# Set-up of a convolution and mixer kernel: the weight on 32 partitions, and iotas between the first two loads of x

## The chip, the cores and the metric

One core of a Trainium2 chip runs the kernel. The metric is the device time of one execution in microseconds, the median of several executions; lower is better.

## The reference

The reference is a light-weight convolution followed by a low-rank token mixer and a two-layer channel mixer. It is cut here to what is computed.

```python
# x: (8, 4224, 192) f32, weight: (8 heads, 7 taps) f32
w = exp(weight - weight.max(-1, keepdims=True))
w = w / (w.sum(-1, keepdims=True) + 1e-9)             # softmax over the 7 taps
out[b, s, h, g] = sum_k w[h, k] * x_pad[b, s + k, h, g]    # causal, 6 zeros in front, 24 channels a head
x = out                                                # (8, 4224, 192)
h = x.transpose(0, 2, 1) @ U @ V                       # U: (4224, 32), V: (32, 4224)
u = x + h.transpose(0, 2, 1)
ch = maximum(u @ w_ch1, 0.0) @ w_ch2                   # 192 -> 768 -> 192
return u + ch
```

## The kernel before, in words

**The steady part.** x is loaded batch by batch and cast to bf16 on the way. TensorE convolves it: for each head it multiplies by a banded 64 or 32 column matrix that holds the softmax of the taps (`conv`, `conv32`). It then sums with U (`tt_mm`), adds the product with V, and runs the two layers of the channel mixer on groups of eight tiles of 128 tokens (`w1`, line 587, and `w2`, line 614). ScalarE and VectorE take the results out of PSUM. The order of the whole program is written out by hand (`SLOTS`, `LOADS`); each engine runs its instructions in program order.

**The set-up.** The change is in the set-up alone, which covers about the first 10 us. It has three strands that meet in the first convolution.

- *Loads.* SyncE issues the load of `weight` into `w_sb` (line 61), the same 56 numbers on every partition. GpSimd issues the first pieces of x for batch 0: `x_piece(0)` makes two transfers, part r = 0 for partitions 0 to 63 (480 KB as bf16) and part r = 1 for partitions 64 to 127 (504 KB), both at line 79. U, the other pieces of x, V and the mixer's weights are issued behind them on GpSimd's queue.
- *The bands.* GpSimd makes four index patterns with `iota` (lines 104 and 114): `dif`, `tap`, `fp` and `efp`. VectorE adds the quarter's offset `rq` to `dif` (line 180), takes the maximum of `w_sb` over the taps (`mx_sb`, 184) and the difference (`d_sb`, 186). ScalarE makes the exponential (193). VectorE compares `dif` with `tap` (`hot`, 195), makes the identity from `fp` (`ident`, 202), finishes the softmax (206 to 212) and multiplies it into the pattern (`pr`, 222, two halves of four heads). TensorE sums each half over the taps with the identity (`band_half`, line 246), and ScalarE (first half) and VectorE (second half) copy the sums into the two `bands`.
- *TensorE's filler.* `idle(4)`, four float32 matmuls of zeros (line 163), runs ahead of the first `band_half`, and `idle(1, 2)` between the two halves.

The first convolution follows at line 379. Its matmuls go r = 0, r = 0, r = 1, r = 1, and so on for each head, so the third of them needs the second transfer of x and the lower half of the first band. `x_zero(0, ...)` clears 64 partitions of row 0 of the tile of x; the convolution reads them as the zeros in front of the sequence.

VectorE also makes `Eq` (line 231) from `efp` and a second column of `rq`, which holds -4 times the first, and `R4` from `fp`; they serve the layout of U (line 274) and later sums.

Of the kernel before, what the change touches and what calls it, by code (L numbers as in the profile page):

```python
# [7 lines left out]
ALU = mybir.AluOpType  # L8
ACT = mybir.ActivationFunctionType
BF16 = mybir.dt.bfloat16  # L10
F32 = mybir.dt.float32
# [3 lines left out]
def kernel(  # L15
# [10 lines left out]
    nc = tc.nc  # L26
    P = nc.NUM_PARTITIONS
    B, S, D = x.shape
    H, KC = weight.shape
# [11 lines left out]
    QB = 32  # L41
# [3 lines left out]
    cst = ctx.enter_context(tc.tile_pool(name="cst", bufs=1))  # L45
# [10 lines left out]
    def bank():  # L56
        return psp.tile([P, 512], F32, name="ps", tag="ps")


    w_sb = cst.tile([P, H, KC], F32, name="w_sb")  # L60
    nc.sync.dma_start(out=w_sb[:], in_=weight[:].partition_broadcast(P))
    xt = [None] * B
    yt = [None] * B

# [5 lines left out]
    def x_tile(b):  # L70
        xt[b] = xs.tile([P, NB1 + 1, D], BF16, name="x_sb")

    def x_zero(b, eng):
        eng.memzero(xt[b][0:HB, 0, :])

    def x_part(b, r, s0, s1):

        blk = NB0 * r + s0 - 1
        return nc.gpsimd.dma_start(  # L79
            out=xt[b][HB * r : HB * r + HB, s0:s1, :],  # L80
            in_=x[b, blk * HB : (blk + s1 - s0) * HB, :].rearrange("(j p) d -> p j d", p=HB),
        )
# [2 lines left out]

    KP = [{0: (0, 10), 1: (0, 10)}, {1: (10, NB1 // 2)}, {0: (10, NB0 // 2)}]

    def x_piece(k):
        for r, (k0, k1) in KP[k].items():
            x_part(0, r, (1 - r if k0 == 0 else 2 * k0 + 1), 2 * k1 + 1)  # L90

    def piece_tiles(k):
        return [NB0 // 2 * r + j for r, ks in KP[k].items() for j in range(*ks)]

    x_tile(0)
    x_piece(0)


    I32 = mybir.dt.int32
# [3 lines left out]
    def iota(t, pattern, base, mul):  # L103
        nc.gpsimd.iota(
            t, pattern=pattern, base=base, channel_multiplier=mul,
            allow_small_or_imprecise_dtypes=True,
        )

    dif = cst.tile([P, BW], F32, name="dif")
    iota(dif[:], [[1, BW]], 0, -1)  # L110
    tap = cst.tile([P, KC], F32, name="tap")
    iota(tap[:], [[-1, KC]], HW, 0)
    fp = cst.tile([P, P], I32, name="fp")
    nc.gpsimd.iota(fp[:], pattern=[[1, P]], base=P, channel_multiplier=-1)
    efp = cst.tile([P, 4, P], F32, name="efp")
    iota(efp[:], [[-1, 4], [1, P]], 0, -4)

# [6 lines left out]
        out=Ur[:, 0:nfull, :], in_=U4[0 : nfull * P, :].rearrange("(k p) c -> p k c", p=P)  # L124
# [3 lines left out]
    for k in range(1, len(KP)):  # L128
        x_piece(k)
# [5 lines left out]
    for q in range(4):  # L135
        src = moe_V[:, 0 : full * 8 * P].rearrange("r (k q t) -> r k q t", q=4, t=2 * P)
        nc.gpsimd.dma_start(
            out=V_sb[32 * q : 32 * q + 32, 0 : 2 * full, :].rearrange(
                "r (k a) t -> r k (a t)", a=2
            ),  # L140
            in_=src[:, :, q, :],
        )
    W1_sb = cst.tile([P, 3, M4], BF16, name="W1_sb")
    for hf in range(2):
        nc.gpsimd.dma_start(
            out=W1_sb[HB * hf : HB * hf + HB, :, :],
            in_=moe_w_ch1[:, :].rearrange("(c k) m -> k c m", k=HB),
# [2 lines left out]
    zz = cst.tile([P, P], F32, name="zz")  # L150
    nc.vector.memzero(zz[:])  # L151

    rq = cst.tile([P, 2], F32, name="rq")
    for r in range(4):
        nc.vector.memset(rq[QB * r : QB * r + QB, 0:1], float(QB * r))
    nc.vector.tensor_scalar(
        out=rq[:, 1:2], in0=rq[:, 0:1], scalar1=-4.0, scalar2=None, op0=ALU.mult
    )
    wps = bank()

    def idle(n, w=4):
# [14 lines left out]
    bands = [cst.tile([P, HQ, P], BF16, name=f"band{hh}") for hh in range(2)]  # L176
    for hh in range(2):
        nc.vector.memzero(bands[hh][:])
    x_zero(0, nc.vector)
    nc.vector.tensor_scalar(  # L180
        out=dif[:], in0=dif[:], scalar1=rq[:, 0:1], scalar2=None, op0=ALU.add
    )
    mx_sb = cst.tile([P, H], F32, name="mx_sb")
    nc.vector.tensor_reduce(out=mx_sb[:], in_=w_sb[:], axis=mybir.AxisListType.X, op=ALU.max)
    d_sb = cst.tile([P, H, KC], F32, name="d_sb")
    nc.vector.tensor_tensor(
        out=d_sb[:],
        in0=w_sb[:],
        in1=mx_sb[:].unsqueeze(2).to_broadcast([P, H, KC]),
        op=ALU.subtract,  # L190
    )
    e_sb = cst.tile([P, H, KC], F32, name="e_sb")
    nc.scalar.activation(e_sb[:], d_sb[:], ACT.Exp)
    hot = cst.tile([P, KC, BW], BF16, name="hot")
    nc.vector.tensor_tensor(
        out=hot[:],
        in0=dif[:].unsqueeze(1).to_broadcast([P, KC, BW]),
        in1=tap[:].unsqueeze(2).to_broadcast([P, KC, BW]),
        op=ALU.is_equal,
    )  # L200
    ident = cst.tile([P, P], BF16, name="ident")
    nc.vector.tensor_scalar(
        out=ident[:], in0=fp[:], scalar1=float(P), scalar2=None, op0=ALU.is_equal
    )
    s_sb = cst.tile([P, H], F32, name="s_sb")
    nc.vector.tensor_reduce(out=s_sb[:], in_=e_sb[:], axis=mybir.AxisListType.X, op=ALU.add)
# [6 lines left out]
        out=c_sb[:].rearrange("p k h -> p h k"),  # L213
        in0=e_sb[:],
        in1=rs_sb[:].unsqueeze(2).to_broadcast([P, H, KC]),
        op=ALU.mult,
    )
    prs = []
    for hh in range(2):
# [3 lines left out]
            out=pr[:],  # L223
            in0=hot[:].unsqueeze(2).to_broadcast([P, KC, HQ, BW]),
            in1=c_sb[:, :, HQ * hh : HQ * hh + HQ].unsqueeze(3).to_broadcast([P, KC, HQ, BW]),
            op=ALU.mult,
# [2 lines left out]

    Eq = cst.tile([P, 4, P], BF16, name="Eq")  # L230
    nc.vector.tensor_scalar(
        out=Eq[:], in0=efp[:], scalar1=rq[:, 1:2], scalar2=None, op0=ALU.is_equal
    )

    nc.vector.tensor_scalar(
        out=fp[:], in0=fp[:], scalar1=R - 1, scalar2=None, op0=ALU.bitwise_and
# [3 lines left out]
        out=R4[:], in0=fp[:], scalar1=0.0, scalar2=None, op0=ALU.is_equal  # L240
# [493 lines left out]
    for r, (k0, k1) in KP[2].items():  # L734
        j = NB0 // 2 * r + k0
        nc.gpsimd.tensor_copy(
            out=U4_sb[:, o : o + k1 - k0, :, :],
            in_=U_sb[:]
# [8 lines left out]
        out=V_sb[0:32, 2 * (NT // 8), :], in_=moe_V[:, (NT - 1) * P : NT * P]  # L747
# [35 lines left out]
    for r in range(4):  # L783
        q = slice(QB * r, QB * r + QB)
        for hh in range(2):
            nc.gpsimd.tensor_copy(
                out=band2[q, HQ * hh : HQ * hh + HQ, :],
                in_=bands[hh][q, :, HB * (r % 2) : HB * (r % 2) + QB],
# [34 lines left out]
    for gs1, gs2, at in SLOTS:  # L823
# [13 lines left out]
        for p in range(npc + 1):  # L837
            for what in at.get(p, []):
                do(what)
            if p < npc:  # L840
                g, k = gs2[p // 4], p % 4
# [35 lines left out]
```

## Time and profile before

| | us |
|---|---|
| median of 3 executions | 324.3 (324.24 to 325.69) |
| the profiled execution | 324.34 |
| its span in the profile | 322.4 |
| TensorE busy | 316.4 (98% of the span) |
| VectorE busy | 268.9 (83%) |
| ScalarE busy | 169.6 (53%) |
| GpSimd busy | 141.8 (44%) |
| mean rate of the transfers | 166 GB/s |

Times in the profile are microseconds from the start of the span unless marked ns. PE is TensorE's matmul, PEld its weight load, DVE VectorE, ACT ScalarE, POOL GpSimd and SP SyncE; POOLq and SPq are the queues that issue transfers. A group in the timeline gives its start, its busy time, the engine, the line, the operation, what it writes and reads, the count, and in brackets the idle time ahead of it with what ended it. The profiled execution takes 1.94 us more than its span.

### The profile page before, as it was taken

The page shows a single profiled execution, that of the slowest core. Times are in us where ns is not written, and L with a number is a line of the kernel's source. Part 1 is how long each engine was busy: PE and PEld are TensorE (multiplying, and loading weights), DVE is VectorE, ACT ScalarE, POOL GpSimd, SP SyncE. Part 2 cuts the span into 40 slices and gives each one's busy share as a digit, 9 for nine tenths or more (in the row PEclk, how much of TensorE's full clock was granted, in tenths as well). Part 3 has the DMA queues.
Part 4 walks back from the last instruction along what each step waited for, and adds up shares of the span by engine and source line. Part 5 has one row for each costly group of instructions (what it writes and reads, how often), then busy time and mean ns, then how long its engine had stood idle before and what let it go on. Part 6 is the DMA issues. An engine that isn't in the chain of part 4 may idle for free.

```text
span 322.4 us, 9590 instructions
## 1 busy us (share of the span) xinstructions
PE 316.4 (98%) x4004; PEld 223.3 (69%) x4004; DVE 268.9 (83%) x550; ACT 169.6 (53%) x344; POOL 141.8 (44%) x108
## 2 busy tenths in 40 slices
PE   8999999999999999999999999999999999999996
PEld 3757576478678647867864884687797497487495
DVE  6769989987977986997898699789888897896864
ACT  1766723960874397088249609824903902912910
POOL 8763299429937983992897497000000000000000
PEclk9999999999999999999999999999999999999999
DMA  8999994999997999799689966138269059039035
GB/s 103 191 195 169 200 226 104 213 179 243 190 188 142 266 151 191 151 185 190 170 230 187 188 171 173 51 107 232 59 177 264 3 148 292 5 97 291 7 121 174
DMA packets 122442, 53.38 MB, mean 166 GB/s; under 512 B 87712, under 2 KB 122400, under 8 KB 122400
## 3 DMA queue, kind: packets, MB, share of 16 engines
q1 hardware_dynamic: 84528, 38.08, 47.4%
q0 software_dynamic: 37728, 14.60, 39.3%
q8 instruction: 31, 0.51, 0.7%
q10 hardware_dynamic: 144, 0.10, 0.1%
q14 instruction: 11, 0.09, 0.1%
HBM read 29.22 MB, written 25.95 MB: 171 GB/s over the span
## 4 chain that ended last, share of the span: by engine, by line
PE 91%; ACT 4%; DMA 2%; DVE 2%; issue 1%; POOL 0%; POOLq 0%
PE ps L614 42%; PE ps L587 39%; PE ps L349 3%; PE ps L469 3%; DMA x_sb<-in_x_dram 2%; PE ps L412 2%; ACT rl_sb L601 2%; ACT y_sb L266 2%; PE ps L379 1%; DVE u_sb L492 1%; DVE rl_sb L603 1%; PE ps L438 0%; PE ps L534 0%; POOL x_sb L79 0%; DVE out_sb L623 0%
## 5 line engine op out<-in xcount | busy, mean ns | idle before, releaser
L601 ACT ACTIVATE rl_sb<-ps 128x512 bf16<-128x512 f32 x233 | 124.3, 604 | 107.7 <-PE ps L587 95.7
L614 PE MATMUL ps<-W_sb,rl_sb 128*128 128x192 bf16 x1584 | 141.2, 246 | 0.2
L614 PEld LDWEIGHTS <-rl_sb 128*128 128x128 bf16 x1584 | 128.3, 98 | 11.8 <-issue 11.4
L587 PE MATMUL ps<-uT,W_sb 64*128 64x512 bf16 x1188 | 131.7, 376 | 0.3 <-DVE uT L268 0.2
L603 DVE TENSOR_SCALAR rl_sb<-ps 128x512 bf16<-128x512 f32 x163 | 105.3, 687 | 14.9 <-PE ps L587 14.7
L587 PEld LDWEIGHTS <-W_sb 64*128 64x128 bf16 x1188 | 66.8, 94 | 60.7 <-issue 4.0
L623 DVE TENSOR_TENSOR out_sb<-ps,u_sb 128x384 f32<-128x384 f32 (+1 forms) x133 | 70.3, 549 | 25.5 <-PE ps L614 25.0
L315 POOL COPY xb_sb<-x_sb 32x3072 bf16<-32x3072 bf16 (+1 forms) x24 | 67.7, 2822 | 1.1
L492 DVE TENSOR_TENSOR u_sb<-y_sb,ps 128x192 bf16<-128x192 bf16 (+1 forms) x168 | 66.2, 460 | 0.0
L303 POOL COPY xb_sb<-x_sb 128x3072 bf16<-128x3072 bf16 x12 | 32.9, 2744 | 39.5 <-PE ps L349 32.4
L266 ACT ACTIVATE y_sb<-ps 128x384 bf16<-128x384 f32 (+4 forms) x90 | 38.3, 519 | 9.8 <-PE ps L349 7.4
L79 POOL DMA_DIRECT2D x_sb<-in_x_dram x32 | 27.1, 853 | 13.9 <-PE ps L469 7.7
L268 DVE CAST y_sb<-ps 128x408 bf16<-128x408 f32 (+4 forms) x36 | 19.1, 577 | 1.4 <-PE ps L379 1.3
L469 PE MATMUL ps<-tt_sb,V_sb 32*128 32x192 bf16 x264 | 12.4, 246 | 0.1
L349 PE MATMUL ps<-x_sb,band 64*32 64x384 bf16 x192 | 12.1, 333 | 0.0
L349 PE MATMUL ps<-xb_sb,band 64*32 64x384 bf16 x192 | 12.1, 332 | 0.0
L469 PEld LDWEIGHTS <-V_sb 32*128 32x128 bf16 x264 | 4.7, 92 | 7.3 <-issue 7.3
L426 ACT ACTIVATE tt_hi<-ps 128x192 bf16<-128x192 f32 x8 | 2.6, 331 | 11.9 <-PE ps L412 11.9
L379 PE MATMUL ps<-x_sb,band 64*64 64x240 bf16 (+3 forms) x192 | 7.9, 275 | 0.5 <-DMA x_sb<-in_x_dram 0.4
L349 PEld LDWEIGHTS <-band 64*32 64x32 bf16 x384 | 4.5, 89 | 5.2 <-issue 2.4
L163 PE MATMUL ps<-zz 128*128 128x512 f32 (+1 forms) x10 | 6.5, 804 | 1.1 <-DVE zz L151 1.1
L379 PEld LDWEIGHTS <-band 64*64 64x64 bf16 x192 | 6.0, 106 | 2.2 <-issue 1.6
(65 smaller groups left out, 67.9 us busy)
## 6 DMA issues: line engine op xcount, KB each, us to landing
out_dram<-out_sb SPq DMA_DIRECT2D x131, 192.0 KB, 2.7
x_sb<-in_x_dram POOLq DMA_DIRECT2D x14, 384.0 KB, 7.6
x_sb<-in_x_dram POOLq DMA_DIRECT2D x7, 432.0 KB, 8.3
x_sb<-in_x_dram POOLq DMA_DIRECT2D x7, 408.0 KB, 7.8
W_sb<-in_moe_w_ch_dram POOLq DMA_DIRECT2D x3, 288.0 KB, 7.5
x_sb<-in_x_dram POOLq DMA_DIRECT2D x1, 504.0 KB, 7.5
uT<-u_sb SPq DMA_TRANSPOSE x31, 4.2
x_sb<-in_x_dram POOLq DMA_DIRECT2D x1, 480.0 KB, 5.7
```

Of the source, the lines that this page charges most:

```text
L79: return nc.gpsimd.dma_start(out=xt[b][HB * r : HB * r + HB, s0:s1, :], in_=x[b, blk * HB : (blk + s1 - s0) * HB, :].rearrange("(j p) d -> ...
L266: nc.scalar.activation(out=out, in_=in_, func=ACT.Copy)
L303: nc.gpsimd.tensor_copy(out=xbt[b][:, s0:s1, :], in_=xt[b][:, s0 + 1 : s1 + 1, :])
L315: nc.gpsimd.tensor_copy(out=xbt[b][q, s0:s1, :], in_=xt[b][q, s0:s1, :])
L349: nc.tensor.matmul(out=pp[r][QB * cg : QB * cg + QB, 0 : nk[r] * GS], lhsT=w[hr], rhs=t[hr, st : st + 2 * nk[r] - 1 : 2, hs], start=True, ...
L469: last = nc.tensor.matmul(out=banks[pr][:, a * D : (a + 1) * D], lhsT=V_sb[32 * q : 32 * q + 32, (j // 8) * 2 + j % 2, :], rhs=ttb[b][32 * ...
L492: nc.vector.tensor_tensor(out=u_group(g)[:, i : i + n, :, hf, :], in0=yt[b][:, run[0] : run[0] + n, :].rearrange("p n (c k) -> p n c k", c=3),
L587: last = nc.tensor.matmul(out=pps[m][hf][:], lhsT=W1_sb[HB * hf : HB * hf + HB, c, m * P : (m + 1) * P], rhs=uTt[g][HB * hf : HB * hf + HB ...
L601: nc.scalar.activation(out=rl[:, m, hf, :], in_=pp[hf][:], func=ACT.Relu)
L603: nc.vector.tensor_scalar_max(out=rl[:, m, hf, :], in0=pp[hf][:], scalar1=0.0)
L614: last = nc.tensor.matmul(out=cps[:, a * D : (a + 1) * D], lhsT=rlt[g][:, m, hf, (i + a) * P : (i + a + 1) * P], rhs=W2_sb[:, m, :], start ...
L623: nc.vector.tensor_tensor(out=o[:, 0:n, :].rearrange("p n (c k) -> p n c k", c=3), in0=cps[:, 0 : n * D].rearrange("p (n c k) -> p n c k", ...
```

## The change

The load of `weight` goes to 32 partitions instead of 128. The maximum runs on 32 partitions. The subtraction is written four times, each time from the same 32 partitions into one quarter of `d_sb`. The two first transfers of x are no longer issued back to back: between them GpSimd makes `fp`, `dif` and `tap` (now in this order) and clears the row of zeros, which VectorE did before; `efp` stays behind both. On VectorE the identity moves ahead of the maximum, and the addition to `dif` moves behind the subtractions. The second column of `rq` goes, with the instruction that made it; `Eq` multiplies by -0.25 in its own instruction and compares with the first column.

```diff
-    w_sb = cst.tile([P, H, KC], F32, name="w_sb")
-    nc.sync.dma_start(out=w_sb[:], in_=weight[:].partition_broadcast(P))
+    w_sb = cst.tile([QB, H, KC], F32, name="w_sb")
+    nc.sync.dma_start(out=w_sb[:], in_=weight[:].partition_broadcast(QB))
...
-    def x_piece(k):
+    def x_piece(k, rs=(0, 1)):
         for r, (k0, k1) in KP[k].items():
+            if r not in rs:
+                continue
             x_part(0, r, (1 - r if k0 == 0 else 2 * k0 + 1), 2 * k1 + 1)
...
     x_tile(0)
-    x_piece(0)
+    x_piece(0, (0,))
...
+    fp = cst.tile([P, P], I32, name="fp")
+    nc.gpsimd.iota(fp[:], pattern=[[1, P]], base=P, channel_multiplier=-1)
     dif = cst.tile([P, BW], F32, name="dif")
     iota(dif[:], [[1, BW]], 0, -1)
     tap = cst.tile([P, KC], F32, name="tap")
     iota(tap[:], [[-1, KC]], HW, 0)
-    fp = cst.tile([P, P], I32, name="fp")
-    nc.gpsimd.iota(fp[:], pattern=[[1, P]], base=P, channel_multiplier=-1)
+    x_zero(0, nc.gpsimd)
+    x_piece(0, (1,))
     efp = cst.tile([P, 4, P], F32, name="efp")
     iota(efp[:], [[-1, 4], [1, P]], 0, -4)
...
-    rq = cst.tile([P, 2], F32, name="rq")
+    rq = cst.tile([P, 1], F32, name="rq")
     for r in range(4):
         nc.vector.memset(rq[QB * r : QB * r + QB, 0:1], float(QB * r))
-    nc.vector.tensor_scalar(
-        out=rq[:, 1:2], in0=rq[:, 0:1], scalar1=-4.0, scalar2=None, op0=ALU.mult
-    )
...
-    x_zero(0, nc.vector)
+    ident = cst.tile([P, P], BF16, name="ident")
+    nc.vector.tensor_scalar(
+        out=ident[:], in0=fp[:], scalar1=float(P), scalar2=None, op0=ALU.is_equal
+    )
+    mx_sb = cst.tile([QB, H], F32, name="mx_sb")
+    nc.vector.tensor_reduce(out=mx_sb[:], in_=w_sb[:], axis=mybir.AxisListType.X, op=ALU.max)
+    d_sb = cst.tile([P, H, KC], F32, name="d_sb")
+    for r in range(4):
+        nc.vector.tensor_tensor(
+            out=d_sb[QB * r : QB * r + QB, :, :],
+            in0=w_sb[:],
+            in1=mx_sb[:].unsqueeze(2).to_broadcast([QB, H, KC]),
+            op=ALU.subtract,
+        )
+    e_sb = cst.tile([P, H, KC], F32, name="e_sb")
+    nc.scalar.activation(e_sb[:], d_sb[:], ACT.Exp)
     nc.vector.tensor_scalar(
         out=dif[:], in0=dif[:], scalar1=rq[:, 0:1], scalar2=None, op0=ALU.add
     )
-    mx_sb = cst.tile([P, H], F32, name="mx_sb")
...
-    d_sb = cst.tile([P, H, KC], F32, name="d_sb")
-    nc.vector.tensor_tensor(
-        out=d_sb[:],
-        in0=w_sb[:],
-        in1=mx_sb[:].unsqueeze(2).to_broadcast([P, H, KC]),
-        op=ALU.subtract,
-    )
...
     hot = cst.tile([P, KC, BW], BF16, name="hot")
...
-    ident = cst.tile([P, P], BF16, name="ident")
...
     Eq = cst.tile([P, 4, P], BF16, name="Eq")
     nc.vector.tensor_scalar(
-        out=Eq[:], in0=efp[:], scalar1=rq[:, 1:2], scalar2=None, op0=ALU.is_equal
+        out=Eq[:],
+        in0=efp[:],
+        scalar1=-0.25,
+        scalar2=rq[:, 0:1],
+        op0=ALU.mult,
+        op1=ALU.is_equal,
     )
```

More of the change, by code (lines that the diff above doesn't have):

```diff
@@ L182 @@
     )
-    mx_sb = cst.tile([P, H], F32, name="mx_sb")
-    nc.vector.tensor_reduce(out=mx_sb[:], in_=w_sb[:], axis=mybir.AxisListType.X, op=ALU.max)
-    d_sb = cst.tile([P, H, KC], F32, name="d_sb")
-    nc.vector.tensor_tensor(
-        out=d_sb[:],
-        in0=w_sb[:],
-        in1=mx_sb[:].unsqueeze(2).to_broadcast([P, H, KC]),
-        op=ALU.subtract,
-    )
-    e_sb = cst.tile([P, H, KC], F32, name="e_sb")
-    nc.scalar.activation(e_sb[:], d_sb[:], ACT.Exp)
     hot = cst.tile([P, KC, BW], BF16, name="hot")
@@ L199 @@
         op=ALU.is_equal,
-    )
-    ident = cst.tile([P, P], BF16, name="ident")
-    nc.vector.tensor_scalar(
-        out=ident[:], in0=fp[:], scalar1=float(P), scalar2=None, op0=ALU.is_equal
     )
```

## The prediction

> **What bounds the kernel now.** I read the head of the page first, for the whole; then the chain of waits over the first 40 us, because the change touches only the set-up; then the timeline of the first 14 us, to see what stands beside that chain; last the transfers in the first 10 us.
>
> ```profile
> span 322.4 us, 9590 instructions
> PE 316.4 (98%) x4004; PEld 223.3 (69%) x4004; DVE 268.9 (83%) x550; ACT 169.6 (53%) x344; POOL 141.8 (44%) x108
> ```
>
> TensorE is busy for 98% of the span. Nothing behind the set-up changes, so whatever the set-up gains or loses shifts the end by that much, and by no more. The chain in order of time (start, length, what) says what the set-up waits for:
>
> ```profile
> 1.26 1.02 POOL x_sb L79
> 2.29 7.50 DMA x_sb<-in_x_dram
> 9.79 0.04 issue
> 9.83 0.53 PE ps L379 x12
> ```
>
> The second transfer of x (r = 1) is issued at 2.29 and lands at 9.79; the convolution goes on at 9.83. The bands, on which most of the edits bear, are not on the chain. The timeline shows by how little:
>
> ```profile
> 0.75 0.40 SPq L61 DMA_DIRECT2D w_sb<-in_weight_dram  x1
> 1.07 5.90 PE L163 MATMUL ps<-zz 128*128 128x512 f32 x8 [1.07 <-DVE zz L151]
> 3.55 0.85 DVE L180 TENSOR_SCALAR dif<-dif,rq 128x38 f32<-128x38 f32 x1 [1.39 <-POOL dif L104]
> 3.74 0.62 POOL L104 IOTA efp<- 128x512 f32 x1
> 4.03 0.37 DVE L184 TENSOR_REDUCE mx_sb<-w_sb 128x8 f32<-128x56 f32 x1
> 6.05 2.44 DVE L222 TENSOR_TENSOR pr<-hot,c_sb 128x1064 bf16<-128x1064 bf16 x2
> 7.37 0.62 PE L246 MATMUL ps<-pr,ident 128*128 128x152 bf16 x7 [0.39 <-DVE pr L222]
> 9.10 0.29 PE L379 MATMUL ps<-x_sb,band 64*64 64x240 bf16 x2
> 9.83 1.83 PE L379 MATMUL ps<-x_sb,band 64*64 64x240 bf16 x62 [0.44 <-DMA x_sb<-in_x_dram]
> ```
>
> The first two matmuls of the convolution run at 9.10, as soon as the upper half of the first band is there; the other 62 stand until 9.79. The bands are ready about 0.6 us before the data.
>
> The transfers from 0 to 10 us, in 40 slices of 0.25 us:
>
> ```profile
> DMA  0000000000004899999999999999999999999999
> GB/s 0 0 0 0 0 0 0 18 20 19 16 4 53 68 99 104 106 158 195 190 190 187 195 183 178 177 184 175 184 197 195 192 192 195 190 188 175 182 183 183
> q1 hardware_dynamic: 144, 0.03, 1.2%
> ```
>
> The slices from 1.75 to about 3 us hold only the weight: the same view cut at 3.0 us has 94 of its 144 packets, cut at 3.7 us it has all. x begins at about 3.0 and needs until 4.5 to come to some 187 GB/s; from there the engines are full. The two transfers of x go one behind the other: part r = 0 lands at 6.96 (5.7 us after its issue, by the page), part r = 1 2.83 us later, and its 504 KB (516 thousand bytes) over 2.83 us are 182 GB/s, the full rate.
>
> **The two transfers of x with the iotas between them.** Part r = 0 is issued at 1.26 as before. Between them come three iotas and the clearing. The starts of `dif`, `tap`, `fp` and `efp` in the trace (3.31, 3.45, 3.55, 3.74) give 0.14 + 0.10 + 0.19 = 0.43 us; GpSimd's own clearing of that shape takes 0.20 at 12.74, and some 0.09 lies ahead of the first iota. The second issue moves from 2.29 to about 3.0. That costs nothing as long as part r = 0 keeps the engines busy: the first packets of r = 0 appear about 1.7 us after its issue, so those of r = 1 would be ready at about 4.7, and the view cut at 6.4 us shows 1293 packets, just past the 1280 rows of r = 0. Cover: 1.7 us. If it failed, the cost is at most the 0.7 us of the move. All that is issued behind (U, the other pieces) moves by the clearing alone, 0.2 us, behind a queue that is full for far longer.
>
> **The weight on 32 partitions.** 128 rows become 32. The first 68 packets had left by 2.5 us, in some 0.7 us, so 32 need about 0.35 and land between 2.5 and 2.9 rather than at 4.05 (issued at 0.75, landed 3.3 us later). The upper bound is 4.05, no gain. By the Trainium skill, "DMA: Bandwidth & Descriptors", section "Rules for kernel authors", a transfer under 64 KB is paid mostly as overhead; by that 28 KB and 7 KB land at nearly the same time, and the maximum would still start near 4.0.
>
> A side effect could matter more. Up to 3.7 us the weight's packets run beside x. Against 187 GB/s, x's start loses 0.65 us x 117 GB/s = 76 KB from 3.0 to 3.65 (70 GB/s there), 0.55 x 85 = 47 KB to 4.2 (102 GB/s), 0.3 x 33 = 10 KB to 4.5 (154 GB/s): 133 KB, or 0.71 us of landing time. Only the first 76 KB, 0.41 us, lie beside the weight; the rest is lost after it has gone, which speaks for a slow start of x's own. So the gain is between nothing and 0.71 us, and I take half of the part beside the weight, 0.2 us. Every transfer behind it, in the same queue, lands earlier by that too.
>
> **VectorE's strand.** Before, from the maximum to `pr` it is 6.05 - 4.03 = 2.02 us. Added: three more subtractions at the 0.14 us that passed from `d_sb` to `hot` (4.46 to 4.60), so 0.42, and `dif` at the 0.15 of the column of `rq`; taken out: the identity, 0.14 (4.94 to 5.08). That makes 2.45 us, and the identity itself fits between the end of `fp` at about 2.65 and the weight. With the maximum at 2.8, `pr` starts at 5.25 and its first half ends at 6.47, before the filler ends at 6.97 (1.07 + 5.90). With the maximum at 4.03, `pr` starts at 6.48.
>
> `dif` took 0.85 us for 38 columns where the row of `rq` took 0.15; it ended at 4.40, with `efp` on GpSimd (3.74 to 4.36). In its new place, near 3.8, it meets the moved `efp` (about 3.95 to 4.6) again; waiting that out moves `pr` from 5.25 to 5.95 and its first half's end to 7.17. The Trainium skill, "SBUF — State Buffer", section "SBUF: two separate sides", calls the port pair of VectorE and GpSimd an exclusive lock that blocks the loser for a whole instruction; this row looks like that, and by the rule the collision is the case to expect.
>
> The first `band_half` then starts between 6.97 and 7.80 (before 7.37), and the first two convolution matmuls could go between 8.7 and 9.5 (before 9.10). Even the late end is ahead of 9.79, so on this path the edits are worth nothing unless r = 1 lands earlier. The second band is less covered: VectorE copies it from 9.21 to 10.51, and the fifth head is due half-way through the convolution, at about 10.75. The late end moves the copy to 10.94; `Eq` with two operations may take up to twice its 0.39 us spacing, another 0.39. That is 0.2 to 0.6 us beyond 10.75 in the worst case. With the weight early the strand leads by 0.4 or more, and the cost is nothing; I take nothing. The column of `rq` and the clearing, taken off VectorE before 2.2 us, stood ahead of 1.39 us of idle time: nothing. In its new place the clearing ends at 3.0, long before the first convolution.
>
> **What ends last further on.** The chain goes on with the other pieces of x at 13.12 and the mixer's weights: `w1` begins at 19.89. These transfers stand in the same queue as x, so they come forward when x does, and stay when it stays.
>
> Sum for the profiled execution: 324.34 - 0.2 = 324.1 us; its time is within 0.04 us of the median.
>
> **The rivals.** *The start of x is its own* (27%): the weight's packets were not in its way, r = 1 lands at 9.79, and all the rest is hidden; 324.3 us. For it: 47 + 10 KB of the loss come after the weight has gone. Against: the weight runs through most of the slow stretch.
>
> *The second transfer comes too late* (18%, slower): full rate comes at 4.2 to 4.5, one microsecond after r = 1's issue ends at 3.22. If one transfer alone gets only some 105 GB/s and it takes the second to fill the engines, the full rate comes 0.7 us later, and r = 1 lands 0.7 x (187 - 105)/187 = 0.3 us later; if a gap opens between the two, by the whole 0.7. That gives 324.65 to 325.0. It decides from the point at which r = 1's first packets come after 6.4 us, or the ramp stretches beyond 4.5. Against it: the slow start is gradual, not a plateau of one transfer.
>
> *A wait that I do not see, or TensorE's clock* (5%, slower): with the bands earlier TensorE stands idle for up to 1.1 us (8.7 to 9.8) where it stood 0.44. The row of the windows from 7 to 10 us has a granted clock of 1.00 with 2.11 us of 3.00 busy; were half the clock granted from there, the 3.0 us of matmuls from 9.83 to 13 would cost some 3 us: 327. An execution like the second of the three shown (325.69) would look alike.
>
> *A larger gain* (2%): r = 0's first packets themselves come forward, when the weight is out of the way. The bands bound it: they are ready at about 8.7 at best, so 9.79 - 8.7 = 1.1 us, 323.2.
>
> **How the numbers follow.** Forecast: 324.1 us, with 48%, for gains of 0.1 to 0.7. The range takes in the start's bounds (323.6) and a little scatter below them, the unchanged case, and the second transfer's worst 0.7 above: 323.5 to 325.0; outside lie the clock and the largest gain. Faster or slower by over 0.5% (1.6 us, about what a measurement of this kernel can tell from no change) needs something outside the set-up's sum: faster 0.02, since even the largest gain stays below it; slower 0.05, the clock's case; same 0.93.
>
> **What would show it.** Right: the convolution's 62 matmuls still wait for the transfer of x, the first bands are ready at about 8.7, the maximum starts before 3.0, and r = 1 lands between 9.1 and 9.8. The step on the start of x is wrong if the ramp still lasts until 4.5 with the weight gone; that on the cover is wrong if the rate of the transfers dips near 6.4 us; that on VectorE if the convolution waits for a band. The whole is wrong if anything behind 20 us has changed by more than a shift.

## The result, and the profile after

The changed kernel takes 325.91 us (median of 19 executions, 325.02 to 328.01) beside 324.68 us (324.21 to 326.07, 19 executions) for the kernel before, run in turn with it. The ratio is 1.0042 [1.0027, 1.0058]. The forecast of 324.1 us had the wrong sign: the change costs 1.2 us instead of saving 0.2, and the time lies above the range. It is within the 0.5% that the forecast called "same", but the interval reaches past that bound.

The profiled execution took 325.36 us, 1.02 more than the one of before, and its span is 1.2 us longer. The head of its page:

```profile
span 323.6 us, 9593 instructions
PE 315.5 (97%) x4004; PEld 224.2 (69%) x4004; DVE 269.5 (83%) x551; ACT 169.5 (52%) x344; POOL 141.7 (44%) x109
```

TensorE worked 0.9 us less in a span 1.2 us longer. Of the 0.9, 0.72 is its filler, which took 5.18 us here and 5.90 before and ended ahead of the bands; the rest of the longer span is waiting. The chain of waits in order of time (start, length, what) says where:

```profile
1.26 1.02 POOL x_sb L79
...
2.38 0.26 POOL fp L112
2.64 0.13 POOL dif L106
2.77 0.10 POOL tap L106
2.87 0.04 POOL x_sb L74
2.91 7.38 DMA x_sb<-in_x_dram
10.30 0.04 issue
10.34 0.53 PE ps L385 x12
...
17.82 0.42 issue
...
20.59 1.32 PE ps L593 x10
```

The three iotas and the clearing are now on the chain. The second transfer of x is issued at 2.91 instead of 2.29, takes 7.38 us instead of 7.50, and lands 0.51 us late. The transfers from 0 to 10 us, in slices of 0.25 us, show why it needed that long although its bytes should have been waiting in the queue:

```profile
DMA  0000000000007989999999999999999999999999
GB/s 0 0 0 0 0 0 0 18 11 0 0 2 54 57 91 115 146 189 189 184 186 190 194 192 169 129 128 126 166 181 178 174 180 181 178 185 163 157 157 169
```

The start of x is as slow as before (full rate at 4.25). From 6.25 to 7.0, where part r = 0 ends and r = 1 takes over, the rate is 126 to 129 GB/s; then it comes back to about 178 until 9.0. Before, these slices held 175 to 197. The 9 in the DMA row stands for 90% or more and hides the rest: from 6.5 to 7.0 us the summed time of the packets is 1.19 times that of the 16 engines, where it was 1.55 before. From 6.5 to 6.75 us 84 packets start where 124 did, and the median packet takes 51 ns in both. So fewer packets run, and the median one is no slower. The timeline shows that the bands were not the cause:

```profile
2.67 0.62 DVE L181 TENSOR_SCALAR ident<-fp 128x128 bf16<-128x128 int32 x1 [0.71 <-POOL fp L112]
2.82 0.47 DVE L185 TENSOR_REDUCE mx_sb<-w_sb 32x8 f32<-32x56 f32 x1
3.35 0.87 DVE L188 TENSOR_TENSOR d_sb<-w_sb,mx_sb 32x56 f32<-32x56 f32 x4
5.98 2.44 DVE L223 TENSOR_TENSOR pr<-hot,c_sb 128x1064 bf16<-128x1064 bf16 x2
9.03 0.29 PE L385 MATMUL ps<-x_sb,band 64*64 64x240 bf16 x2
10.34 1.83 PE L385 MATMUL ps<-x_sb,band 64*64 64x240 bf16 x62 [1.02 <-DMA x_sb<-in_x_dram]
```

The first two convolution matmuls run at 9.03, almost where they ran before. The other 62 wait 1.02 us for x, where they waited 0.44.

**Where the 1.2 us of span went.** The late landing is 0.51. At `w1` the lag is 0.70 (20.59 against 19.89), because the issue gap behind the first matmul of line 723 is 0.42 where it was 0.23. The last block of `w2` starts 0.96 later (308.18 against 307.22), and 0.24 follows behind it. The 0.26 between `w1` and that block is not a fixed cost of the change. A second execution of the same kernel (`e7_changed_again`, below) has x 0.79 late, `w1` only 0.45 late (20.34), and that block 1.08 late (308.30). The wait of 6.6 us for a transposed `u` at 41 us, which this trace has and that one has not, does not decide it either. From `w1` to that block it is 287.33 us before, 287.59 and 287.96 in these two, and 288.43 in e5 below, which has no late x. Executions of the kernel before differ by more (324.2 to 326.1). So the two profiles trace 0.45 to 0.70 us, at `w1`, of the 1.2 us between the medians; where the rest arises is not shown.

### The profile page after: what moved, and what is told of

It is laid out like the page before. It is cut to its first block, busy times and chain, and to the rows that moved or that the text cites. A ratio compares the mean times of both kernels' runs of the same rounds, so it can differ in the third digit from the quotient of the medians.

```text
span 323.6 us, 9593 instructions
## 1 busy us (share of the span) xinstructions
PE 315.5 (97%) x4004; PEld 224.2 (69%) x4004; DVE 269.5 (83%) x551; ACT 169.5 (52%) x344; POOL 141.7 (44%) x109
## 4 chain that ended last, share of the span: by engine, by line
PE 89%; DMA 4%; ACT 3%; DVE 2%; issue 1%; POOL 0%; POOLq 0%
PE ps L620 40%; PE ps L593 39%; PE ps L355 3%; PE ps L475 3%; DMA x_sb<-in_x_dram 2%; DMA uT<-u_sb 2%; PE ps L418 2%; ACT rl_sb L607 2%; ACT y_sb L272 2%; PE ps L385 1%; DVE u_sb L498 1%; DVE rl_sb L609 1%; PE ps L540 0%; POOL x_sb L79 0%; PE ps L444 0%
## 5 line engine op out<-in xcount | busy, mean ns | idle before, releaser
L593 PEld LDWEIGHTS <-W_sb 64*128 64x128 bf16 x1188 | 67.7, 94 | 59.9 <-issue 3.7
L418 PE MATMUL ps<-y_sb,U_sb 128*32 128x192 bf16 x258 | 7.4, 247 | 0.0
```

What stands on the lines that cost most here:

```text
L593: last = nc.tensor.matmul(out=pps[m][hf][:], lhsT=W1_sb[HB * hf : HB * hf + HB, c, m * P : (m + 1) * P], rhs=uTt[g][HB * hf : HB * hf + HB ...
```

## The experiments: which half of the change costs the time

Theory A: the second load of x is issued too late, and the transfers lose rate for it. Theory B: the weight on 32 partitions and VectorE's new order disturb x or the bands. Three kernels split the change.

**Loads together again** (the changed kernel, less the split):

```diff
-    x_piece(0, (0,))
+    x_piece(0)
...
-    x_piece(0, (1,))
```

> The changed kernel with both first loads of x issued back to back again, ahead of the iotas; the weight on 32 partitions, the four subtractions and VectorE's new order stay. Theory A (the later issue of the second transfer makes it land late): the transfers show no dip between 6.0 and 7.3 us, the second transfer lands at 9.8 or a little before (10.30 in the changed kernel, 9.79 before), and the time is that of the kernel before, ratio 0.998 to 1.001. Theory B (the weight's smaller load or VectorE's new order disturbs x): the dip and the ratio of about 1.004 stay.

Measured: 324.95 us (324.91 to 326.37), ratio 1.0015 [1.0004, 1.0026], a little more than expected. Its transfers from 0 to 10 us:

```profile
GB/s 0 0 0 0 0 0 0 17 12 0 0 0 65 71 91 69 92 164 184 187 194 194 197 194 186 185 195 186 195 192 194 190 195 195 194 185 175 182 185 180
```

The dip is gone and x lands at 9.65. What is left of the loss goes with VectorE in this profile: with the identity ahead of the maximum and behind late iotas, `pr` starts at 7.28, and the fifth head waits for its band until 11.80. The changed kernel has no such delay (`pr` at 5.98).

**Iotas between, all else as before** (the kernel before, with the split):

```diff
-    x_piece(0)
+    x_piece(0, (0,))
...
+    fp = cst.tile([P, P], I32, name="fp")
+    nc.gpsimd.iota(fp[:], pattern=[[1, P]], base=P, channel_multiplier=-1)
     dif = cst.tile([P, BW], F32, name="dif")
     iota(dif[:], [[1, BW]], 0, -1)
     tap = cst.tile([P, KC], F32, name="tap")
     iota(tap[:], [[-1, KC]], HW, 0)
-    fp = cst.tile([P, P], I32, name="fp")
-    nc.gpsimd.iota(fp[:], pattern=[[1, P]], base=P, channel_multiplier=-1)
+    x_zero(0, nc.gpsimd)
+    x_piece(0, (1,))
...
-    x_zero(0, nc.vector)
```

> The kernel before with one part of the change alone: three iotas and the clearing between the two first loads of x. The weight on 128 partitions and VectorE's order stay as before. Theory A: the dip near 6 to 7 us appears, the second transfer lands near 10.3, ratio near 1.004. Theory B: no dip, 9.8, ratio 1.000.

Measured: 325.44 us, ratio 1.0030 [1.0017, 1.0044]. Its transfers from 0 to 10 us:

```profile
GB/s 0 0 0 0 0 0 0 18 20 20 19 23 64 63 98 95 126 160 174 178 194 192 184 194 181 125 91 103 127 149 167 174 178 172 174 178 174 169 172 165
```

The same dip at the same place, deeper (91 GB/s), with the weight still on 128 partitions. x lands at 10.97.

**The weight on 32 partitions alone** (the kernel before, with the smaller load and the four subtractions):

```diff
-    w_sb = cst.tile([P, H, KC], F32, name="w_sb")
-    nc.sync.dma_start(out=w_sb[:], in_=weight[:].partition_broadcast(P))
+    w_sb = cst.tile([QB, H, KC], F32, name="w_sb")
+    nc.sync.dma_start(out=w_sb[:], in_=weight[:].partition_broadcast(QB))
...
-    mx_sb = cst.tile([P, H], F32, name="mx_sb")
+    mx_sb = cst.tile([QB, H], F32, name="mx_sb")
...
+    for r in range(4):
+        nc.vector.tensor_tensor(
+            out=d_sb[QB * r : QB * r + QB, :, :],
...
```

> The kernel before with the weight loaded on 32 partitions and four subtractions, and nothing else. Theory A: the second transfer lands at 9.7 to 9.8, ratio 0.999 to 1.000. Theory B: near 10.3 and ratio near 1.004.

Measured: 324.72 us, ratio 1.0007 [0.9996, 1.0018]. Its transfers:

```profile
GB/s 0 0 0 0 0 0 0 18 11 0 0 2 55 52 71 101 121 163 180 194 195 189 195 194 187 180 181 195 194 194 194 192 194 194 194 185 177 182 183 185
```

There is no dip, and x lands at 9.78. The bands come late here (below), and the median still hardly moves. A holds: the dip comes and goes with the split of the loads, and the split alone gives most of the loss. B falls for x. VectorE's new order costs something only where the identity waits for late iotas (e1), and it does not in the changed kernel.

## The experiments: what about the split

**How long a separation?** Four kernels move the second load to other instants; the first is issued at 1.26 or 1.27 in each. e5, the kernel before with only the clearing between:

```diff
-    x_piece(0)
+    x_piece(0, (0,))
+    x_zero(0, nc.gpsimd)
+    x_piece(0, (1,))
...
-    x_zero(0, nc.vector)
```

> The kernel before with only the clearing of x's zero row on GpSimd between the two first loads of x (some 0.1 to 0.2 us), no iota. Theory A1 (any break between the two requests gives the second a slow start of its own): the transfers dip below 170 GB/s between 6.0 and 7.5 us, the convolution waits 0.8 us or more for x, the second transfer lands at 10.2 to 11.0, ratio 1.002 to 1.004. Theory A2 (an iota between the requests is what hurts): no dip, landing at 9.8 to 9.9, ratio 1.000 to 1.0005.

e6, the kernel before with the iota `tap` alone between:

```diff
-    x_piece(0)
+    x_piece(0, (0,))
...
-    dif = cst.tile([P, BW], F32, name="dif")
-    iota(dif[:], [[1, BW]], 0, -1)
     tap = cst.tile([P, KC], F32, name="tap")
     iota(tap[:], [[-1, KC]], HW, 0)
+    x_piece(0, (1,))
+    dif = cst.tile([P, BW], F32, name="dif")
+    iota(dif[:], [[1, BW]], 0, -1)
```

> The kernel before with the smallest iota alone (tap, 0.1 us and what is ahead of a first iota) between the two first loads of x. Theory A1: dip and landing at 10.2 to 11.0, ratio 1.002 to 1.004. Theory A2: the same. If only a long delay of the request (0.6 us and more) hurts, there is no dip, the landing is 9.8 to 9.9 and the ratio 1.000 to 1.0005, here and with the clearing alone.

e12, the changed kernel with `fp` alone between:

```diff
     nc.gpsimd.iota(fp[:], pattern=[[1, P]], base=P, channel_multiplier=-1)
+    x_piece(0, (1,))
...
     x_zero(0, nc.gpsimd)
-    x_piece(0, (1,))
```

> The changed kernel with only fp's iota between the loads; dif, tap and the clearing follow the second request, which goes out near 2.6. The identity then runs on VectorE while it is issued. Theory C: dip, landing at 10.2 or later. Theory D, with its point between 2.49 and 2.91: no dip or a small one, landing at 9.6 to 9.9. VectorE's dif waits until about 3.8, so the bands are ready near 9.0 to 9.3; ratio 1.000 to 1.001 without the dip, 1.003 with it.

e4, the changed kernel with `efp` between as well:

```diff
-    x_piece(0, (1,))
     efp = cst.tile([P, 4, P], F32, name="efp")
     iota(efp[:], [[-1, 4], [1, P]], 0, -4)
+    x_piece(0, (1,))
```

> The changed kernel with the fourth iota (efp, about 0.55 us more) between the two loads too, so that the second is issued near 3.5 instead of 2.91. Theory A, if the landing follows the issue: the second transfer lands near 10.8, and the time grows by another 0.5 us or so, ratio near 1.006. If only the separation counts and not its length: 10.3 and 1.004. Theory B: no change against the changed kernel, and the dip at the same place.

Measured:

| what stands between | second issue | x lands | ratio |
|---|---|---|---|
| the clearing (e5) | 2.40 | 9.79 | 1.0004 [0.9994, 1.0014] |
| iota `tap` (e6) | 2.49 | 9.81 | 1.0008 [0.9999, 1.0016] |
| iota `fp` (e12) | 2.57 | 10.70 | 1.0014 [1.0000, 1.0028] |
| as changed | 2.91 | 10.30 | 1.0042 [1.0027, 1.0058] |
| `efp` too (e4) | 3.46 | 10.34 | 1.0022 [1.0005, 1.0040] |

Neither a break between the loads nor an iota is enough by itself. The transfers and one line of the timeline of e6, then of e12:

```profile
GB/s 0 0 0 0 0 0 0 18 18 21 20 19 60 75 77 83 120 154 187 190 189 192 192 186 183 178 180 181 190 195 195 195 192 195 192 184 182 178 184 183
9.85 1.83 PE L382 MATMUL ps<-x_sb,band 64*64 64x240 bf16 x62 [0.71 <-DMA x_sb<-in_x_dram]
```

```profile
GB/s 0 0 0 0 0 0 0 17 12 0 0 2 55 80 57 89 91 177 192 190 195 195 195 189 178 177 166 175 180 184 190 190 195 181 160 175 155 165 176 182
10.74 0.50 PE L385 MATMUL ps<-x_sb,band 64*64 64x240 bf16 x12 [1.19 <-DMA x_sb<-in_x_dram]
```

With 1.22 us from issue to issue (e6) there is no dip and no loss clear of the noise. With 1.30 us (e12) x is 0.9 us late in the one profile that was taken, without a dip: from 6.0 to 7.25 the rate stays at 166 or more. The trace holds 16 completion signals for each transfer, and they say what was late. In e12, 15 of the 16 of x's second part come from 9.30 to 9.83 us, as before (9.20 to 9.79), and one comes at 10.70; U's then come by 11.35 but for one at 12.54. In the changed kernel nine come by 9.66 and seven from 9.99 to 10.30. So, as far as these signals tell, a part of the transfer lags and not the whole. That e12's ratio is smaller than this profile suggests speaks for a loss that differs between executions. e4 speaks against "the later, the worse": at 2.20 us its profile loses no more than the changed kernel's at 1.65.

**Is it VectorE or GpSimd's iotas?** Theory C: VectorE's work, running while GpSimd prepares the second transfer, delays it. e9, the kernel before with a clearing of an unused tile between the loads, VectorE being idle meanwhile:

```diff
-    x_piece(0)
+    x_piece(0, (0,))
+    jk = cst.tile([P, 512], F32, name="jk")
+    nc.gpsimd.memset(jk[:], 0.0)
+    x_piece(0, (1,))
```

> The kernel before with one unused fill of 128 x 512 on GpSimd (about 0.5 us) between the two first loads of x and the iotas all behind them, so that the second request goes out near 2.9 while VectorE stands idle, waiting for its first iota. Theory C (VectorE's instructions of the kind that share a port with GpSimd, running while the second request is issued, spoil it): no dip, landing at 9.7 to 9.9, ratio 1.000 to 1.0015 (the bands come 0.5 us later). Theory D (the second request is too late: fine at 2.49, spoilt at 2.91 and after): the dip between 6.0 and 7.3, landing at 10.2 to 11.0, ratio 1.002 to 1.004.

e10, the kernel before with the loads together and VectorE kept busy over their issue:

```diff
     x_zero(0, nc.vector)
+    jk = cst.tile([P, 512], F32, name="jk")
+    nc.vector.memzero(jk[:])
+    jo = cst.tile([P, 512], F32, name="jo")
+    for _ in range(3):
+        nc.vector.tensor_scalar(out=jo[:], in0=jk[:], scalar1=1.0, scalar2=None, op0=ALU.add)
```

> The kernel before, both loads back to back, with one unused fill and three unused float32 additions of 128 x 512 on VectorE from 2.2 us on, in the time in which the second request is issued (2.29 to 3.22). Theory C: dip, the second transfer lands at 10.2 or later. Theory D: no dip, 9.8; if the additions run past 3.55 the bands come a few tenths later, ratio at most 1.001.

e11, the changed kernel with the identity moved back behind `hot`:

```diff
-    ident = cst.tile([P, P], BF16, name="ident")
...
     mx_sb = cst.tile([QB, H], F32, name="mx_sb")
...
+    ident = cst.tile([P, P], BF16, name="ident")
...
     s_sb = cst.tile([P, H], F32, name="s_sb")
```

> The changed kernel with the identity moved back behind hot on VectorE; the loads stay separated, the second request near 2.91. While it is issued (to 3.88) VectorE now runs the maximum and the subtractions alone, as in the kernel with the weight first, which showed no dip. Theory C: no dip, landing at 9.6 to 9.9, ratio 1.000. Theory D: dip, 10.2 to 11.0, ratio 1.003 to 1.004.

The transfers of e9, then of e10, from 0 to 10 us:

```profile
GB/s 0 0 0 0 0 0 0 18 20 20 19 20 74 61 74 84 121 170 190 194 194 192 194 197 178 143 131 135 169 177 175 183 190 187 186 191 166 165 142 160
```

```profile
GB/s 0 0 0 0 0 0 0 18 20 20 19 22 74 73 55 74 115 189 194 186 192 190 195 192 191 181 194 194 194 195 194 194 189 195 194 188 171 182 187 182
```

e9 has the dip without any iota between the loads and with VectorE idle from 2.16 to 4.01 (second issue 2.75, landing 10.46, ratio 1.0034 [1.0015, 1.0054]). e10 has VectorE busy from 2.21 to 5.43 and no dip; x lands at about 9.5. Its ratio of 1.0075 [1.0047, 1.0103] is in part the bands' doing: they are so late that the convolution begins at 10.42 only. That puts `w1` 0.79 us behind the kernel before in its profile; the medians of 6 and 25 executions differ by 2.3, where 0.3 at most was expected, and the rest is not traced. C falls, since the dip is absent here and present in e9. e11 (326.45 us, 1.0044 [1.0028, 1.0061]) keeps the dip and is no better than the changed kernel, so the place of the identity is not the cause either.

**Is it the time since the program's start, or the distance between the two requests?** e13, the kernel before with a fill ahead of both loads:

```diff
+    jk = cst.tile([P, 512], F32, name="jk")
+    nc.gpsimd.memset(jk[:], 0.0)
     x_piece(0)
```

> The kernel before with the unused fill (0.54 us) ahead of both first loads of x, which stay back to back; the iotas follow. The second request then goes out near 2.8, later than the point at which the separated ones were spoilt, but as close behind the first as before. Theory D1 (what counts is the distance to the first request, with its point between 1.23 and 1.31 us from issue to issue): no dip, all shifted by 0.54, landing at 10.3, ratio 1.001 to 1.002. Theory D2 (what counts is the time since the start of the program): dip, landing at 10.8 or later, ratio 1.003 or more.

e14, the kernel before with U's first load between the two:

```diff
-    x_piece(0)
+    x_piece(0, (0,))
...
+    Ur = cst.tile([P, NUB, 4 * R], BF16, name="Ur")
...
+    nc.gpsimd.dma_start(
+        out=Ur[:, 0:nfull, :], in_=U4[0 : nfull * P, :].rearrange("(k p) c -> p k c", p=P)
+    )
+    x_piece(0, (1,))
...
```

> The kernel before with the load of U (256 KB) issued between the two first loads of x: the queue is not left without a new request, but the second part of x is issued near 3.2 to 3.3. It is served 1.4 us later than before in any case, and lands near 11.2, so the time is some 1.4 us more. Theory D1a (the queue must get its next request soon after the first, whichever it is): no dip, landing at 11.1 to 11.3. Theory D1b (a request that comes late behind the first is spoilt itself): dip where the second part of x starts, about 7.5 to 9 us, landing at 11.6 or later. If the lead of a request over its service counts (3.5 us or more were enough, less was not), there is no dip, since the lead is about 4.4 us.

e13 tells nothing: the fill ran from 0.75 to 1.27, in time in which GpSimd waits anyway, and the loads went out at 1.29 and 2.31 (ratio 1.0001 [0.9989, 1.0014]). e14 took 325.29 us in its one execution, 0.6 above the median of the kernel before and not the 1.4 expected. Its transfers, and its chain:

```profile
GB/s 0 0 0 0 0 0 0 18 20 20 19 23 75 48 63 86 141 160 186 194 195 194 194 194 186 173 175 183 178 185 178 179 197 195 195 194 192 190 192 194
```

```profile
2.27 0.90 POOL Ur L103
3.17 7.86 DMA x_sb<-in_x_dram
11.03 0.04 issue
```

x's second part is issued at 3.17, later than in the changed kernel, and there is no dip (173 GB/s at the least from 6 us on). It lands at 11.03 because U's 256 KB stand ahead of it. So, by this one profile, a late request for x is not slow in itself: with another request 1.01 us behind the first, the rate holds. All the runs fit a limit on the distance from the first request to the next on GpSimd's queue. It lies above 1.22 us (e6) and below 1.49 us (e9), and below 1.30 if e12's single profile is taken for the same effect; e12 differs from e6 in the weight and in VectorE's order too. A limit on how long a request must stand before its bytes are due is not excluded: in e14 U's bytes come due first, so x's second part stands in the queue for longer. Nor is it excluded that GpSimd's other work between the requests does it, since no run leaves GpSimd idle there. No run here separates these, and the cause inside stays open.

## The experiments: the clock, and the way back

**The changed kernel again**, unchanged, one execution:

> The changed kernel once more, for a second profile. If the slow start of the second transfer belongs to the kernel: a dip near 6 to 7 us again and a landing of 10.2 to 11.0. If it was chance in the first profile: no dip and 9.7 to 9.8. The wait for a transposed u near 41 to 48 us (0.5 us more than before) may or may not be there; if it comes and goes with one kernel, it is scatter and no effect of the edits.

Measured: 325.5 us; second issue 2.91, landing 10.58, a dip to 98 GB/s. The dip is there in each of the two profiles and its size varies.

**TensorE's clock.** e11's profiled execution has more than the dip. Its windows (stretch, length, busy time and count of PE, PEld, DVE, ACT and POOL, granted clock, share of the DMA engines, GB/s):

```profile
9.30:10.80 1.50, 0.00 (x0) 0.00 (x0) 1.00 (x4) 0.00 (x0) 0.00 (x0) 1.00 1.53 154
10.80:13.50 2.70, 2.65 (x66) 2.29 (x69) 1.32 (x2) 2.10 (x5) 1.36 (x3) 0.66 1.62 188
13.50:16.00 2.50, 2.50 (x51) 1.84 (x52) 1.41 (x3) 1.11 (x3) 1.93 (x4) 0.68 1.49 192
```

After 1.62 us without a matmul the granted clock is 0.66 and 0.68 over the next 5.2 us; the 62 convolution matmuls take 2.65 us instead of 1.83, and `w1` begins at 21.91, 2.0 us behind the kernel before. The late landing is 1.0 of that (10.81 against 9.79), and the clock about the other 1.0. Executions with a mean clock of 0.995 or less were 3 of 8 of e11, 4 of 19 of the changed kernel (327.04 to 328.01 us), 2 of 12 of e2, 1 of 12 of e9, and none of the 106 of the kernel before that ran in turn with the experiments (0.998 at the least). The changed kernel's slow end is not the clock's alone: two executions of 327.23 and 327.64 us have a clock of 1.00, and without the four the median is 325.78 instead of 325.91. The wait does not decide it alone: e2's profile waits 1.79 us at a clock of 1.00.

One kernel gave TensorE more filler in that wait:

```diff
     band_half(1)
+    idle(1)
```

> The changed kernel with one more filler matmul of 512 columns on TensorE behind the second half of the bands (about 1.3 us, from about 9.0 to 10.3). It leaves the late landing of x as it is. If TensorE's clock falls in part of the executions of the changed kernel (4 of 19 had a mean granted clock of 0.993 to 0.995, at 327.0 to 328.0 us) because TensorE stands idle ahead of the convolution, no execution here has a mean clock under 0.997 and none is over 327; median 325.4 to 325.9, ratio 1.003 to 1.004. If the falls have another cause, about one in five still shows it.

Measured: 326.25 us (325.67 to 327.3, 6 executions), ratio 1.0047 [1.0028, 1.0065], above the 325.4 to 325.9 expected. The clock stayed at 0.999 or above in all six; the slowest took 327.3 us at a clock of 1.00, so long executions do not need the clock's fall. At a rate of 4 in 19, six without a fall would happen by chance about once in four (0.79 to the sixth power is 0.24), and the time did not improve. So the filler settles nothing, and it is no remedy: the transfer is still late (landing 10.74).

**The weight first, the loads together.** The changed kernel with the two loads together, the iotas in the old order, the clearing back on VectorE, the identity behind `hot`, and the maximum and the subtractions first on VectorE:

```diff
-    x_piece(0, (0,))
+    x_piece(0)
...
-    x_zero(0, nc.gpsimd)
-    x_piece(0, (1,))
...
-    ident = cst.tile([P, P], BF16, name="ident")
...
+    x_zero(0, nc.vector)
     mx_sb = cst.tile([QB, H], F32, name="mx_sb")
...
```

> Both first loads of x back to back and the iotas behind them in their old order, the weight on 32 partitions, and on VectorE the maximum and the four subtractions ahead of the addition to dif, the identity behind hot. The weight lands near 2.2, so maximum and subtractions (0.21 us each, by the runs so far) are done by 3.4, in time that VectorE spent idle; dif waits for GpSimd's iotas until 4.4 as before, and pr starts at 5.7 to 5.9 (6.05 before, 7.09 to 7.28 where the subtractions stood behind the iotas). The second transfer lands at 9.6 to 9.8 without a dip. Ratio 0.999 to 1.000: nothing lost, and at most 0.2 us won, since the landing of x is the bound. If the four subtractions cost by themselves wherever they stand, ratio 1.001.

Its chain, and the maximum in its timeline:

```profile
1.25 1.02 POOL x_sb L79
2.27 7.31 DMA x_sb<-in_x_dram
9.58 0.04 issue
9.62 0.53 PE ps L384 x12
```

```profile
2.58 0.20 DVE L180 TENSOR_REDUCE mx_sb<-w_sb 32x8 f32<-32x56 f32 x1 [0.51 <-DMA w_sb<-in_weight_dram]
```

Measured: 324.24 us (323.97 to 325.42), ratio 0.9998 [0.9986, 1.0009]. It undoes the loss. It is not measurably faster than the kernel before: the maximum starts 1.45 us earlier, `pr` starts at 6.02 (5.7 to 5.9 expected, 6.05 before), and the end waits for x as it did.

## Why the prediction was wrong

- **The step that failed** is the one on the second transfer's cover: "That costs nothing as long as part r = 0 keeps the engines busy", with "Cover: 1.7 us". Counting packets was right in itself, r = 0 did keep the engines busy until past 6 us. The unstated assumption was that a request that is issued before it is needed then runs at full rate. Instead the rate was 126 to 129 GB/s for 0.75 us at the hand-over, and x landed at 10.30 instead of 9.79. In the profiles with the two loads apart the cost was 0.5 to 1.2 us of landing time, against "at most the 0.7 us of the move", and 0.2 to 1.0 us of it was left at `w1` (e11, with the clock's fall, set aside). The term stood in the sum at nothing. What in the queue makes the late request slow stays open.
- **The rival that had the place and the sign**, "the second transfer comes too late", was given 18%, but neither of its deciding points was met. The ramp ended at 4.25, and by 6.4 us 1342 packets of the queue had started against the 1280 of r = 0, so r = 1 had begun. The sign that the forecast itself named for the step on the cover, a dip of the rate near 6.4 us, is what the trace shows. The rival's price of 0.3 to 0.7 fits what the two profiles have at `w1` (0.45 and 0.70) but is too small for the medians. The clock's falls explain 0.13 us of the difference; the rest is not traced.
- **The gain on x's start**, 0.2 us, is not shown. The 0.25 us slices from 3.0 to 4.5 sum to 588 before and 652 after, which is 16 KB; as the 588 hold the last 50 packets of the weight, about 10 KB, x itself is 26 KB or 0.14 us ahead. But with the weight on 32 partitions and the loads together they sum to 552, 563 and 581 (e1, e3, e8), a lead of 1 to 8 KB. There x landed at 9.65, 9.78 and 9.58, and with the weight on 128 partitions and no dip at 9.79, 9.79, 9.81 and 9.51 (before, e5, e6, e10). So "the start of x is its own" was right on this point, within the scatter of single profiles.
- **The weight** came a little earlier than said: 7 KB on 32 rows land 1.7 us after the issue, at 2.44, where 28 KB on 128 rows took 3.3. The Trainium skill's rule ("DMA: Bandwidth & Descriptors", section "Rules for kernel authors") that transfers under 64 KB are mostly overhead would, as the prediction used it, have had them land alike; the measurement decides against that use of it. Rows and bytes both fell to a quarter, so which of them counted is not shown.
- **VectorE's strand** was right by its end, for partly wrong reasons. `pr` started at 5.98 (said 5.25, or 5.95 with the collision). The four subtractions took 0.87 where the one before took 0.22, so that the three added ones cost 0.65 and not 0.42. The addition to `dif` took 0.40 from its start to that of `hot`, where 0.15 was said, and the identity and the maximum took 0.62 and 0.47 beside GpSimd's work (0.30 and 0.37 before). The feared collision of `dif` with `efp` cost no whole iota, because `dif` began only at 4.25. Whether there was a wait is open: `dif` ended 0.04 us behind `efp` (4.54 and 4.50), as it did before (4.40 and 4.36), but its 0.29 us is also what it took in e11, where `efp` began only as it ended. In e3 the four subtractions stand behind the addition to `dif`, as the one did before. There `pr` starts at 7.09 instead of 6.05: 0.75 of it is the subtractions (5.35 - 4.46 up to `hot`, 0.14 before), and 0.27 an instruction on `s_sb` that took 0.44 instead of 0.17. `Eq` with two operations cost nothing (spacing 0.40 against 0.39).
- **The clock's case**, given 5% with a price of 3 us, does occur, in 4 of 19 executions by the mean clock, and costs about 1.0 us in e11's profile. It was set up to follow from earlier bands; the runs show it together with the later x. The Trainium skill ("TensorE: Matmul & The Clock Gate", section "Why this matters for your kernels") asks to avoid idle gaps over about 3 us; here 1.62 us was followed by the lower clock, so staying under that figure was no protection.
- **The steady part** was said to pass on the set-up's shift "and by no more". That is not shown: from `w1` to the last block of `w2` the kernel before takes 287.33 us and the changed one 287.59 and 287.96, and e5, whose x is on time, takes 288.43. This scatter is as large as the effect.

## What to carry to other kernels

A transfer that is "covered" by the queue ahead of it is covered only if it also runs at full rate when its turn comes; that needs a row of its own in the trace, and a dip at the hand-over is the place to look. At the program's start, some 0.3 us or more of GpSimd's work between its first two load requests cost 0.5 to 1.0 us in the medians of e2, e4, e9 and e12, although the first load was still running; with the iotas behind both (e8) the loss was gone. This is no rule for any two requests: in the kernel before, U's stands 2.0 us behind x's second (4.29 and 2.29) with four iotas between them, and the rate at that hand-over, from 9.0 us on, is 175 to 183 GB/s. When an engine needs a transfer and a computed operand, and the operand is ready 0.6 us ahead of the transfer, speeding up the operand is worth nothing until the transfer moves.

## What the runs showed of the hardware that was not expected

- Two requests on GpSimd's queue at the program's start, 1.22 us apart at most: full rate at the hand-over (178 to 195 GB/s in e6). At 1.30 us and more, in seven kernels, x was 0.5 to 1.2 us late; in six of them the lowest slices from 6.0 to 7.25 us were 91 to 155 GB/s, and in the seventh (e12, 1.30 us) one of 16 completion signals was late. With another request in between (e14, one profile) the two parts of x stood 1.91 us apart and no dip came.
- The granted clock fell to 0.66 behind 1.62 us without a matmul in e11's profile, and stayed at 1.00 behind 1.79 us in e2's.
- A write of 32 partitions into a quarter of a tile takes VectorE 0.20 to 0.21 us for 56 columns (e3); the whole 128 partitions in place took 0.22.
